# Changes of order and placement in a clustered-attention and SwiGLU kernel: casts of two heads, group and border order, table load, last output tile

## The chip, the cores and the metric

The kernel runs on one core of a Trainium2 chip. A core has five engines that run their own instruction streams in order and wait for each other on semaphores: TensorE (PE in the profile; its weight loads are shown as PEld), VectorE (DVE), ScalarE (ACT), GpSimd (POOL) and SyncE (SP), which here only issues DMAs. The metric is the time of one execution on the device, in microseconds. Lower is better.

## The reference

Attention over 4 batches, 8 heads, 768 tokens and 64 dimensions, restricted to pairs of tokens that fall into the same of 16 clusters, and behind it a normalised SwiGLU feed-forward layer:

```python
q_assign = argmax(einsum('bhsd,hcd->bhsc', q_n, c_n))
k_assign = argmax(einsum('bhsd,hcd->bhsc', k_n, c_n))
scores = where(q_assign[..., None] == k_assign[:, :, None, :], scale * q @ k^T, -1e9)
attn = softmax(scores) @ v
x = attn, heads side by side                  # 3072 x 512
xn = x / sqrt(mean(x*x) + 1e-6) * rms_g
out = (silu(xn @ w_gate) * (xn @ w_val)) @ w_out   # d_ff 1536
```

All inputs and the output are float32; the large products run in bf16.

## The kernel before

**Units and groups.** The 3072 tokens are cut into 8 *units* of 384 query tokens (half a batch each, three tiles of 128). Unit `u` goes through attention over 8 heads, then a norm, then the feed-forward layer. The 32 (batch, head) pairs are prepared in 8 *groups* of four heads: `trans` (L200) transposes q or k of one head on PE and evacuates it as `qkT` (ACT, or DVE for group 2); `cast` (L218) writes it as bf16 into `qext` or `kext`; `cluster_steps` (L254) finds the cluster of each token as one-hot rows, and `place` (L276) writes these rows by DMA below the 64 dimensions of `qext`/`kext`. A score product over 64 + 16 rows is then the scaled score plus a large number where the clusters agree; an exp with a bias takes the rest to zero. In the first two groups the one-hot rows are written by a DVE transpose instead (`pair_clusters`, `under`; `head(n)` does k and q of head `n`), and `cast` writes every second column there.

**Stages.** While unit `u` is in attention, PE also does feed-forward work of units `u-1` and `u-2` and transposes of a later group. `attention` (L591) walks over the 24 gaps of a unit (8 heads, three score chunks each): it issues the scores of a chunk (two 384-column matmuls and one exp on ACT), the product with v of the previous head (`pv`, L322, once per head; every second head DVE takes a reciprocal and writes `x`, which frees the accumulator), any hook for that gap, and then items from a list `fill`, spread by their costs. In unit 0 the hooks (`first`, with `gap1`, `gap5` and so on) carry the preparation of groups 0 to 2 instead. `gap5` (L565) has POOL cast k and q of heads 6 and 7; `head(6)` and `head(7)` follow in gaps 10 and 13, the transposes of group 2 (`late`, evacuated by DVE) in gaps 14 to 21. `second_batch` issues input loads on SP behind a small DMA (`hold`) that waits for a reciprocal of unit 0.

**The feed-forward work** of a unit (`ffn_work`) is four x transposes `xtrans` (L371; three PE transposes each, DVE writes `xnT`) and 12 pairs of gate and val (`gv`, L382): four 384-column matmuls each; ACT makes tanh of the gate, DVE two more steps (`th`, `gvT`); the last unit uses ACT's Silu and one DVE step. `out_work` is nine parts, three for each of three output tiles `o` (`out_mm`, L407; four 512-column matmuls per part), then ACT copies the tile to `o_sb` and SP issues its DMA. `border` puts the four x transposes of one unit between the last parts of the output work of the unit before. `CUT` leaves the last 8 of the 24 gate and val items of a unit to the start of the next unit.

**What sets the order.** The program is written in order by hand; each engine runs its instructions in that order. All transposes, gates, vals, cluster products and output tiles share three PSUM buffers (`ps_g`), scores have two, `pv` one. An instruction that needs a buffer waits for the engine that reads the oldest one.

**Behind the last attention gap** stand, in order: the last `pv`; the 8 left-over gates and vals of unit 6; the norm of unit 7 (three squares on ACT, a chain of small DVE steps, three DVE multiplications `xn`); the output of unit 6 with the x transposes of unit 7; gates and vals of unit 7; its output, whose last tile is copied in two halves by DVE and by ACT.

Of the kernel before, what the change touches and what calls it, by code (L numbers as in the profile page):

```python
# [9 lines left out]
F32 = mybir.dt.float32  # L10
# [4 lines left out]
ACT = mybir.ActivationFunctionType  # L15
# [7 lines left out]
def kernel(  # L23
# [12 lines left out]
    nc = tc.nc  # L36
    B, H, S, D = q.shape
# [238 lines left out]
    def place(on, g, m):  # L276

        ext = (kext if m else qext)[g % 4]
        for h in range(HG):
            for e in range(2):  # L280
                on.dma_start(out=ext[D:D + NC, h, e * UQ:(e + 1) * UQ],  # L281
                             in_=put[g, m][32 * h + e * NC:32 * h + (e + 1) * NC])
# [39 lines left out]
    def pv(u, h):  # L322
        b, _, nt = UNITS[u]
        g, hh = b * 2 + h // HG, h % HG
        if h == 0:
            xs[u] = xp.tile([P, HT, DM], F32, tag="x", name="x", bufs=2)
        if h % 2 == 0:
            accs[u] = ps_a.tile([P, 2, HT, D + 1], F32, tag="acc", name="acc")
        acc = accs[u]
        for t in range(nt):  # L330
            for kc in range(ST):
                nc.tensor.matmul(acc[:, h % 2, t], lhsT=pT[u, h][:, kc, t * P:(t + 1) * P],  # L332
                                 rhs=vbf[g % 4][:, hh, kc % HT * 2 + kc // HT], start=kc == 0, stop=kc == ST - 1)
        if h % 2:
            inv = small.tile([P, 2, HT], F32, tag="inv", name="inv")
            invs[u] = inv
            nc.vector.reciprocal(inv[:, :, :nt], acc[:, :, :nt, D])
            dst = xs[u][:, :nt, (h - 1) * D:(h + 1) * D].rearrange("p t (h d) -> p h t d", d=D)
            nc.vector.tensor_tensor(dst, acc[:, :, :nt, :D],
                                    inv[:, :, :nt].unsqueeze(3).broadcast_to([P, 2, nt, D]), op=ALU.mult)  # L340
# [63 lines left out]

    outs = {}

    def out_mm(u, t, part):  # L407
        b, col, _ = UNITS[u]
        if part == 0:
            outs[u] = ps_g.tile([P, DM], F32, tag="gen", name="o")  # L410
        for f in range(4 * part, 4 * part + 4):
            nc.tensor.matmul(outs[u], lhsT=gvT[u][:, f, t * P:(t + 1) * P], rhs=wo[:, f], start=f == 0, stop=f == FC - 1)  # L412
        if part == 2:
            o = outp.tile([P, DM], F32, tag="o_sb", name="o_sb")
            rows = out[b * S:(b + 1) * S].rearrange("(p t) f -> p t f", t=ST)[:, (col + t) % HT * 2 + (col + t) // HT]
            if (u, t) == (NU - 1, HT - 1):
                c = DM // 2
                nc.vector.tensor_copy(o[:, :c], outs[u][:, :c])
                nc.sync.dma_start(out=rows[:, :c], in_=o[:, :c])
                nc.scalar.copy(o[:, c:], outs[u][:, c:])  # L420
                nc.scalar.dma_start(out=rows[:, c:], in_=o[:, c:])
            else:
                nc.scalar.copy(o, outs[u])  # L423
                nc.sync.dma_start(out=rows, in_=o)


    def group_work(g):

        t, c = [], []
        for h in range(HG):  # L430
            n = g * HG + h
            t += [(0.3, lambda h=h: trans(g, h, 0)), (0.3, lambda h=h: trans(g, h, 1))]

            def others(n=n):
                vcast(n)
                load_qk(n + NQ)
                load_v(n + NV)

            def both(h=h, f=others):
                cast(nc.gpsimd, g, h, 0)  # L440
                f()
                cast(nc.vector, g, h, 1, (0,))
            if g == 2:
                c.append((0.0, others))
            else:
                c += [(0.0, both), (0.0, lambda h=h: cast(nc.vector, g, h, 1, (1,)))]
        a = []
        for m in range(2):
            a += [(0.0 if i else 0.7, f) for i, f in enumerate(cluster_steps(g, m))]
            a.append((0.0, lambda m=m: place(nc.sync if g == 2 else nc.gpsimd, g, m)))  # L450
        return t, c, a

    def group(g):
        t, c, a = group_work(g)
        return [x for h in range(HG) for x in t[2 * h:2 * h + 2] + c[2 * h:2 * h + 2]] + a

    def spread(a, b):

        if not a:
            return list(b)  # L460
        w, n = [], 0
        for i, x in enumerate(a):
            w.append(x)
            while n < len(b) * (i + 1) // len(a):
                w.append(b[n])
                n += 1
        return w

    def ffn_work(u):
        n = UNITS[u][2] / HT  # L470
        w = [(0.18 * n, lambda c=c: xtrans(u, c)) for c in range(CC)]
        for f in range(FC):
            for val in (False, True):
                w.append((0.64 * n, lambda f=f, val=val: gv(u, f, val)))
        return w
# [3 lines left out]

    def border(o, ffn):  # L480

        return o[:-3] + ffn[:2] + o[-3:-2] + ffn[2:3] + o[-2:-1] + ffn[3:4] + o[-1:]


    def tokens(g, h, on=None):
# [3 lines left out]
    def casts(on, n, *what):  # L489
        for m, e in what:  # L490
            cast(on, n // HG, n % HG, m, (e,))
# [39 lines left out]
    def more():  # L531
        busy(1, False)
# [10 lines left out]
    def head(n):  # L543
        under(n, 1)
        under(n, 0)
# [18 lines left out]

    def gap5():  # L565
        pair_clusters(2)
        casts(pool_, 6, K0, K1, Q0)
        casts(pool_, 7, K0, K1, Q0)
        vcast(6)
        vcast(7)  # L570
        load_gv(3)
        for n in (6, 7):
            casts(pool_, n, Q1)
        head(4)

    def gap9():
# [3 lines left out]
    early = [lambda h=h, m=m: trans(1, h, m) for h in (2, 3) for m in (1, 0)]  # L580
    late = [lambda h=h, m=m: trans(2, h, m, nc.vector) for h in range(HG) for m in (1, 0)]
    first = {1: gap1, 2: early[0], 3: early[1], 4: lambda: (early[2](), early[3]()), 5: gap5,
             7: lambda: (more(), head(5)), 9: gap9, 10: lambda: (more(), head(6)), 13: lambda: (more(), head(7))}
    first.update({14 + i: f for i, f in enumerate(late)})
    first[14] = lambda: (late[0](), second_batch())
    first[16] = lambda: (late[2](), casts(pool_, H, K0, Q0, K1, Q1))
# [4 lines left out]
    def attention(heads, fill, skip=0, hooks={}):  # L591
        gaps = [(u, h, i) for u, h in heads for i in range(UNITS[u][2])]
        total, done, n = sum(c for c, _ in fill), 0.0, 0
        for at, (u, h, i) in enumerate(gaps):
            scores(u, h, i)
            if i == min(1, UNITS[u][2] - 1):
                for p in due:
                    pv(*p)
                due[:] = [(u, h)]
            if h == H - 1:  # L600
                squares(u, i, False)
            if (u, h, i) in hooks:
                hooks[u, h, i]()
            while n < len(fill) and at >= skip and done <= total * (at + 1 - skip) / (len(gaps) - skip):
                done += fill[n][0]
                fill[n][1]()
                n += 1
        for _, f in fill[n:]:
            f()

    attention([(0, h) for h in range(H)], [], hooks={(0, *divmod(i, HT)): first.get(i, more) for i in range(H * HT)})
    for u in range(1, NU):
        ffn, o, g = ffn_work(u - 1), out_work(u - 2) if u > 1 else [], u + 2
        if u == 1:
            t, c, a = group_work(2)
            t3, c3, a3 = group_work(3)
            n = 4
            prep = c + a + [x for h in range(HG) for x in t3[max(2 * h, n):2 * h + 2] + c3[2 * h:2 * h + 2]] + a3[:5]
            idle = const.tile([P, 1], BF16)

            def norm():
                rms(0)
                nc.gpsimd.tensor_copy(idle, xn[0][:, HT - 1, DM - 1:])
                for h in range(1, HG):
                    casts(pool_, H + h, K0, Q0, K1, Q1)
                    load_o((h - 1) * FC // 3)

            hooks = {(1, 0, 1): norm}
            hooks.update({(1, *divmod(2 + i, HT)): t3[i][1] if i < n else more for i in range(LEAD - 2)})
            at = (1, *divmod(LEAD - 1, HT))  # L630
            hooks[at] = lambda f=hooks[at]: (f(), busy(4, False))
            fill = ffn[:CC] + spread(ffn[CC:CUT], prep)
            attention([(1, h) for h in range(H)], fill, LEAD, hooks)
        else:
            fill = ffn_work(u - 2)[CUT:] + [(0.0, lambda u=u: rms(u - 1))]
            fill += border(spread(o[:3], a3[5:]) + o[3:], ffn) if u == 2 else border(o, ffn)
            attention([(u, h) for h in range(H)], fill + spread(ffn[CC:CUT], group(g) if g < NG else []), 1)
    pv(NU - 1, H - 1)
    for _, f in ffn_work(NU - 2)[CUT:]:
        f()  # L640
    rms(NU - 1)
    for _, f in border(out_work(NU - 2), ffn_work(NU - 1)) + ffn_work(NU - 1)[CC:] + out_work(NU - 1):
        f()


# [28 lines left out]
```

## Time and profile before

| | |
|---|---|
| median of 6 runs | 355.77 us (355.05 to 356.78) |
| the profiled execution | 356.0 us, span 354.2 us |
| granted PE clock | 0.998 over the span |
| PE busy | 340.5 us (96%) |
| ACT busy | 261.3 us (74%) |
| DVE busy | 222.9 us (63%) |
| POOL busy | 112.5 us (32%), nearly all before 250 us |

The span is the time from the first to the last instruction in the profile; 1.8 us of the execution lie around it. In a row of the timeline or of the chain, the first number is the start in us from the beginning of the span, the second the duration; `x4` is the number of instructions that were merged; a bracket gives the time that the engine was idle before the row and what ended the idle time. `L412` is line 412 of the kernel before. A busy PE is not a PE at its peak: matmuls overlap, so a pause is seen where the distance between two starts is longer than usual. Unit 1 begins near 37.6 us and unit 2 near 79; from border to border a unit takes about 41.4 us while groups are being prepared and 36.9 us after that; the last attention gap is near 310 us.

### The profile page before, as it was taken

To read this page: it belongs to the slowest core of one execution; us is meant where nothing else is said; L and a number is where in the kernel's file an instruction comes from. 1 tells how busy PE (TensorE), PEld (TensorE's weight loads), DVE (VectorE), ACT (ScalarE), POOL (GpSimd) and SP (SyncE) were. 2 spreads that over 40 slices of the span, in tenths; PEclk is the share of its full clock that TensorE was granted. 3 is DMA by queue.
4 is the path that set the end of the run, shared out by engine and by line. 5 is a ranking of instruction groups with operands and counts; after the bars stand their busy time and mean duration, and the time that the engine had idled before them with its cause. 6 is when DMAs were issued, how large, how long until landed. Compare 5 with 4: busy or idle time off the path is not lost.

```text
span 354.2 us, 7973 instructions
## 1 busy us (share of the span) xinstructions
PE 340.5 (96%) x3016; PEld 207.8 (59%) x3033; DVE 222.9 (63%) x549; ACT 261.3 (74%) x458; POOL 112.5 (32%) x226
## 2 busy tenths in 40 slices
PE   7997999999999999999999999999999999999995
PEld 3646656565665557655675656755566656654552
DVE  3887869677568655786368764687546654675430
ACT  5897968987778769787787877878778877852421
POOL 4899586241453403371042801535000000000000
PEclk9999999999999999999999999999999999999999
DMA  7999989273361014501130001000100001001002
GB/s 261 333 227 196 304 155 270 63 219 116 98 192 40 17 59 138 162 16 39 59 92 2 22 32 61 0 9 18 59 31 0 2 35 57 3 0 62 30 2 89
DMA packets 27158, 31.62 MB, mean 89 GB/s; under 512 B 4464, under 2 KB 24176, under 8 KB 27120
## 3 DMA queue, kind: packets, MB, share of 16 engines
q1 hardware_dynamic: 18320, 24.88, 21.2%
q0 software_dynamic: 8368, 5.71, 9.8%
q8 instruction: 24, 0.39, 0.5%
q10 hardware_dynamic: 432, 0.52, 0.4%
q14 instruction: 14, 0.11, 0.1%
HBM read 28.35 MB, written 6.29 MB: 98 GB/s over the span
## 4 chain that ended last, share of the span: by engine, by line
PE 81%; ACT 9%; DVE 3%; DMA 2%; issue 2%; POOL 2%; SPq 0%; ACTq 0%; DVEq 0%; POOLq 0%
PE o L412 17%; PE gate L390 16%; PE val L390 15%; PE s L314 15%; PE acc L332 9%; ACT pT L318 5%; PE tq L206 4%; PE sc L240 3%; DMA qk<-in_q_dram 1%; PE tx L377 1%; ACT th L398 1%; ACT qkT L212 1%; POOL qext L225 1%; ACT xn L357 1%; DMA out_dram<-o_sb 1%
## 5 line engine op out<-in xcount | busy, mean ns | idle before, releaser
L318 ACT ACTIVATE pT<-s,off 128x768 bf16<-128x768 f32 x192 | 171.0, 904 | 36.2 <-PE s L314 35.3
L314 PE MATMUL s<-qext,kext 80*128 80x384 bf16 x384 | 94.8, 327 | 4.2 <-POOL qext L225 1.6
L390 PE MATMUL gate<-xnT,wg 128*128 128x384 bf16 x384 | 78.3, 325 | 0.4 <-DVE gvT L403 0.4
L390 PE MATMUL val<-xnT,wv 128*128 128x384 bf16 x384 | 78.1, 326 | 0.5 <-ACT th L396 0.5
L399 DVE SCALAR_TENSOR_TENSOR th<-th,gate 128x384 f32<-128x384 f32 x84 | 46.5, 554 | 50.2 <-ACT th L398 49.7
L412 PE MATMUL o<-wo,gvT 128*128 128x512 bf16 x271 | 69.2, 378 | 1.2 <-ACT o_sb L423 0.3
L225 POOL CAST qext<-qkT 64x384 bf16<-64x384 f32 x64 | 34.4, 543 | 77.3 <-ACT qkT L212 34.7
L314 PEld LDWEIGHTS <-kext 80*128 80x128 bf16 x384 | 36.9, 98 | 35.8 <-issue 10.7
L398 ACT ACTIVATE th<-gate 128x384 f32<-128x384 f32 x84 | 41.1, 489 | 16.6 <-PE gate L390 16.2
L390 PEld LDWEIGHTS <-wv 128*128 128x128 bf16 x384 | 36.1, 97 | 25.3 <-issue 3.3
L403 DVE SCALAR_TENSOR_TENSOR gvT<-th,val 128x384 bf16<-128x384 f32 x84 | 46.1, 549 | 6.8 <-PE val L390 1.5
L390 PEld LDWEIGHTS <-wg 128*128 128x128 bf16 x384 | 35.8, 97 | 24.1 <-issue 3.1
L332 PEld LDWEIGHTS <-pT 128*128 128x128 bf16 x1152 | 43.6, 97 | 9.3 <-ACT pT L318 0.6
L332 PE MATMUL acc<-vbf,pT 128*128 128x65 bf16 x1152 | 45.7, 193 | 0.5 <-ACT pT L318 0.5
L412 PEld LDWEIGHTS <-gvT 128*128 128x128 bf16 x288 | 26.9, 97 | 26.1 <-issue 0.5
L206 PE MATMUL tq<-ident_f,qk 128*128 128x128 f32 x192 | 31.5, 280 | 1.5 <-DMA qk<-in_q_dram 1.3
L212 ACT ACTIVATE qkT<-tq 128x384 f32<-128x384 f32 x56 | 26.6, 496 | 4.5 <-PE tq L206 4.0
L281 POOL DMA_DIRECT2D qext<-oh x40 | 19.1, 486 | 30.3 <-DVE oh L270 24.3
L206 PEld LDWEIGHTS tq<-ident_f,qk 128*128 128x128 f32 x192 | 23.1, 142 | 9.4 <-DVE gvT L403 1.8
L423 ACT COPY o_sb<-o 128x512 f32<-128x512 f32 x23 | 13.5, 585 | 19.6 <-PE o L412 19.2
L378 DVE TENSOR_SCALAR xnT<-tx,gcol 128x384 bf16<-128x384 bf16 x32 | 12.7, 414 | 22.7 <-PE tx L377 22.5
L281 POOL DMA_DIRECT2D kext<-oh x40 | 19.1, 485 | 11.2 <-DVE xnT L378 10.9
(71 smaller groups left out, 250.9 us busy)
## 6 DMA issues: line engine op xcount, KB each, us to landing
qk<-in_q_dram SPq DMA_DIRECT2D x32, 192.0 KB, 3.9
vs<-in_v_dram SPq DMA_DIRECT2D x32, 192.0 KB, 4.6
out_dram<-o_sb SPq DMA_DIRECT2D x23, 256.0 KB, 2.0
qk<-in_k_dram SPq DMA_DIRECT2D x30, 192.0 KB, 4.1
wg<-in_moe_w_gate_dram POOLq DMA_DIRECT2D x4, 384.0 KB, 7.4
wv<-in_moe_w_val_dram POOLq DMA_DIRECT2D x4, 384.0 KB, 9.1
wo<-in_moe_w_out_dram POOLq DMA_DIRECT2D x3, 512.0 KB, 5.9
qext<-oh POOLq DMA_DIRECT2D x40, 12.0 KB, 1.6
```

Of the source, the lines that this page charges most:

```text
L206: nc.tensor.transpose(ps[:, i * P:(i + 1) * P], qk[:, part, 2 * i:2 * i + 2].rearrange("p t d -> p (t d)"), ident_f)
L212: nc.scalar.activation(to, ps, ACT.Copy, scale=by)
L225: on.tensor_copy(to, of)
L281: on.dma_start(out=ext[D:D + NC, h, e * UQ:(e + 1) * UQ], in_=put[g, m][32 * h + e * NC:32 * h + (e + 1) * NC])
L314: nc.tensor.matmul(ps[:, j, :w] if nt == HT else flat[:, j * w:(j + 1) * w], lhsT=cols(kext[g % 4][:KR, hh], g, kc // HT, kc % HT * P, (kc ...
L318: nc.scalar.activation(pT[u, h][:, n * i:n * i + n, :w], of, ACT.Exp, bias=off, scale=scale * ZS)
L332: nc.tensor.matmul(acc[:, h % 2, t], lhsT=pT[u, h][:, kc, t * P:(t + 1) * P], rhs=vbf[g % 4][:, hh, kc % HT * 2 + kc // HT], start=kc == 0 ...
L390: nc.tensor.matmul(ps, lhsT=w[:, c, f * P:(f + 1) * P], rhs=xnT[u][:, c, :n], start=c == 0, stop=c == CC - 1)
L398: nc.scalar.activation(th, ps, ACT.Tanh, scale=0.5)
L399: nc.vector.scalar_tensor_tensor(th, th, 1.0, ps, op0=ALU.add, op1=ALU.mult)
L403: nc.vector.scalar_tensor_tensor(gvT[u][:, f, :n], gates[u], 0.5, ps, op0=ALU.mult, op1=ALU.mult)
L412: nc.tensor.matmul(outs[u], lhsT=gvT[u][:, f, t * P:(t + 1) * P], rhs=wo[:, f], start=f == 0, stop=f == FC - 1)
```

## The change

Five places of the program are changed.

- k of heads 6 and 7 is cast by DVE behind `head(6)` in gap 10 and `head(7)` in gap 13, instead of by POOL in gap 5.
- For groups 4 to 7, `place` for q no longer stands behind the cluster steps of q; one item behind those of k places both. The list of a group has one entry less, and so the interleave with the gates and vals shifts.
- `border` puts the first part of the third output tile ahead of the x transposes: two transposes follow it, then the second part, two transposes, and the third part.
- One gate of unit 6 is put ahead of the last `pv`. A dummy Silu behind the last norm brings the load of ACT's table there.
- The last output tile is computed in two column halves, each with 12 matmuls of 256 columns in a PSUM tile of its own; ACT copies the first half, DVE the second, and SP issues both DMAs.

```diff
     def out_mm(u, t, part):
...
-            if (u, t) == (NU - 1, HT - 1):
-                c = DM // 2
-                nc.vector.tensor_copy(o[:, :c], outs[u][:, :c])
-                nc.sync.dma_start(out=rows[:, :c], in_=o[:, :c])
-                nc.scalar.copy(o[:, c:], outs[u][:, c:])
-                nc.scalar.dma_start(out=rows[:, c:], in_=o[:, c:])
-            else:
-                nc.scalar.copy(o, outs[u])
-                nc.sync.dma_start(out=rows, in_=o)
+            nc.scalar.copy(o, outs[u])
+            nc.sync.dma_start(out=out_rows(u, t), in_=o)
+
+    def out_half(u, t, half):
+
+        c = slice(half * DM // 2, (half + 1) * DM // 2)
+        to = ps_g.tile([P, DM // 2], F32, tag="gen", name="o")
+        for f in range(FC):
+            nc.tensor.matmul(to, lhsT=gvT[u][:, f, t * P:(t + 1) * P], rhs=wo[:, f, c], start=f == 0, stop=f == FC - 1)
+        o = outp.tile([P, DM // 2], F32, tag="o_sb", name="o_sb")
+        if half:
+            nc.vector.tensor_copy(o, to)
+        else:
+            nc.scalar.copy(o, to)
+        nc.sync.dma_start(out=out_rows(u, t)[:, c], in_=o)
...
             a += [(0.0 if i else 0.7, f) for i, f in enumerate(cluster_steps(g, m))]
-            a.append((0.0, lambda m=m: place(nc.sync if g == 2 else nc.gpsimd, g, m)))
+            if g <= 3:
+                a.append((0.0, lambda m=m: place(nc.sync if g == 2 else nc.gpsimd, g, m)))
+        if g > 3:
+            a.append((0.0, lambda: [place(nc.gpsimd, g, m) for m in range(2)]))
...
     def border(o, ffn):
 
-        return o[:-3] + ffn[:2] + o[-3:-2] + ffn[2:3] + o[-2:-1] + ffn[3:4] + o[-1:]
+        return o[:-2] + ffn[:2] + o[-2:-1] + ffn[2:4] + o[-1:]
...
     def gap5():
         pair_clusters(2)
-        casts(pool_, 6, K0, K1, Q0)
-        casts(pool_, 7, K0, K1, Q0)
+        casts(pool_, 6, Q0)
+        casts(pool_, 7, Q0)
...
-             7: lambda: (more(), head(5)), 9: gap9, 10: lambda: (more(), head(6)), 13: lambda: (more(), head(7))}
+             7: lambda: (more(), head(5)), 9: gap9, 10: lambda: (more(), head(6), casts(nc.vector, 6, K0, K1)),
+             13: lambda: (more(), head(7), casts(nc.vector, 7, K0, K1))}
...
+    rest = ffn_work(NU - 2)[CUT:]
+    rest[0][1]()
     pv(NU - 1, H - 1)
-    for _, f in ffn_work(NU - 2)[CUT:]:
+    for _, f in rest[1:]:
         f()
     rms(NU - 1)
-    for _, f in border(out_work(NU - 2), ffn_work(NU - 1)) + ffn_work(NU - 1)[CC:] + out_work(NU - 1):
+    nc.scalar.activation(first_exp, off, ACT.Silu)
+    for _, f in border(out_work(NU - 2), ffn_work(NU - 1)) + ffn_work(NU - 1)[CC:] + out_work(NU - 1)[:-3]:
         f()
+    for half in range(2):
+        out_half(NU - 1, HT - 1, half)
```

More of the change, by code (lines that the diff above doesn't have):

```diff
@@ L405, with out_rows @@
     outs = {}
+    def out_rows(u, t):
+        b, col, _ = UNITS[u]
+        return out[b * S:(b + 1) * S].rearrange("(p t) f -> p t f", t=ST)[:, (col + t) % HT * 2 + (col + t) // HT]
     def out_mm(u, t, part):
-        b, col, _ = UNITS[u]
         if part == 0:
@@ L414, in out_mm @@
             o = outp.tile([P, DM], F32, tag="o_sb", name="o_sb")
-            rows = out[b * S:(b + 1) * S].rearrange("(p t) f -> p t f", t=ST)[:, (col + t) % HT * 2 + (col + t) // HT]
-            if (u, t) == (NU - 1, HT - 1):
-                c = DM // 2
-                nc.vector.tensor_copy(o[:, :c], outs[u][:, :c])
-                nc.sync.dma_start(out=rows[:, :c], in_=o[:, :c])
-                nc.scalar.copy(o[:, c:], outs[u][:, c:])
-                nc.scalar.dma_start(out=rows[:, c:], in_=o[:, c:])
-            else:
-                nc.scalar.copy(o, outs[u])
-                nc.sync.dma_start(out=rows, in_=o)
+            nc.scalar.copy(o, outs[u])
[11 more added lines that the diff above has]
+        nc.sync.dma_start(out=out_rows(u, t)[:, c], in_=o)
     def group_work(g):
```

## The prediction

> **What bounds the kernel now.** I read the page's shares and chain first, then the chain of waits in order of time near the end, then the timeline of the stretches that the edits touch.
>
> ```profile
> PE 81%; ACT 9%; DVE 3%; DMA 2%; issue 2%; POOL 2%; SPq 0%; ACTq 0%; DVEq 0%; POOLq 0%
> ```
>
> TensorE (PE) is busy for 340.5 of 354.2 us and makes 81% of the chain that ended last. Whatever lies beside it is free; what counts is the short pauses in which PE waits. Start-to-start distances of its matmuls give the pauses: 0.163 us for a 384-column one, 0.2155 us for a 512-column one (22 in 4.92 us of the chain), 0.11 us for an f32 transpose; anything longer is a pause. The end of the chain shows four:
>
> ```profile
> 311.56 0.60 PE acc L332 x14
> ...
> 322.65 0.59 ACT o_sb L423
> 323.24 0.04 issue
> 323.29 1.02 PE o L412 x4
> ...
> 327.08 1.22 issue
> 328.30 0.50 ACT th L396
> 328.80 0.04 issue
> 328.85 0.81 PE val L390 x4
> ...
> 350.46 0.44 DVE o_sb L418
> 350.90 0.02 issue
> 350.92 0.37 ACT o_sb L420
> ```
>
> The last `pv` (`acc`) waits for the last exp; the third output tile waits for a PSUM buffer that ACT's copy frees; a gate waits for the Silu table (1.28 us of the "issue" row); and the two halves of the last copy run one after the other. The timeline of unit 3 has a smaller copy of the second, and one more kind:
>
> ```profile
> 128.32 0.59 ACT L423 COPY o_sb<-o 128x512 f32<-128x512 f32 x1 [0.83 <-PE o L412]
> ...
> 128.95 1.02 PE L412 MATMUL o<-wo,gvT 128*128 128x512 bf16 x3
> ...
> 144.88 0.31 PEld L206 LDWEIGHTS tq<-ident_f,qk 128*128 128x128 f32 x3 [0.37 <-DVE gvT L403]
> ```
>
> PE starts `o` right when the copy ends (128.91), and the transpose right when `gvT` (144.29 + 0.54) frees its buffer. In the head, the edit of the casts meets this:
>
> ```profile
> 30.37 0.31 PEld L206 LDWEIGHTS tq<-ident_f,qk 128*128 128x128 f32 x3 [0.53 <-DVE qkT L210]
> ...
> 30.54 1.31 POOL L225 CAST kext<-qkT 64x384 bf16<-64x384 f32 x2
> ...
> 32.57 0.50 PE L314 MATMUL s<-qext,kext 80*128 80x384 bf16 x2 [1.64 <-POOL qext L225]
> ```
>
> Scores of head 6 wait for POOL. DVE (VectorE) is then already late too: the fourth transpose waited for it until 30.37.
>
> **The change, part by part.** All on the profiled execution: span 354.2 us, its own time 356.0 us (1.8 us around the span), 0.23 above the median 355.77 of the six runs. I subtract the sum from the median.
>
> *Casts of k, heads 6 and 7.* POOL loses four casts (0.61 to 0.65 us each) and could give q of head 6 by 31.2 instead of 32.52. DVE gains four casts of c us: two ahead of the reciprocal at 27.75, two ahead of the `qkT` copy at 29.76. Queued behind the first two: reciprocal and `x`, which free the accumulator for the next `pv` (so PE stands 2c there), the `hold` DMA on SP and the loads behind it. Those land about 1 us later, which is covered: the load of head 12, issued at 28.65, lands 4.1 us later, and its transposes run at 39.8. Behind all four: the copy that frees the buffer of PE's fourth transpose. That transpose starts at 30.38 + 4c, takes 0.33, and the scores of head 6 follow at 30.71 + 4c. Against 32.57 that breaks even at c = 0.465. DVE's own contiguous cast takes 0.355 in most cases, 0.55 and 0.57 at 61.4 and 94.8 where a POOL cast ran beside it (gain 0.4, loss 0.4 us). These casts write every second column; on POOL that costs 0.61 against 0.50. POOL is casting beside the first two (27.50 to 29.13) and part of the others (from 30.54), so I take 0.50: **+0.1 us**, bounds -0.45 and +0.4. From there ACT's exps follow back to back to 40.9, so the shift goes through to the end. POOL's later work (weights issued 2.5 us earlier, first used tens of us later) gates nothing.
>
> [...]
>
> *Group work, units 2 to 5.* `place` of both halves behind the second half's steps leaves POOL's order as it was (eight DMAs of q, then eight of k). But the list is nine entries long instead of ten, so the interleave with gates shifts: by the instruction order the last head's two transpose triples stand together behind the gate, and on DVE `gvT` no longer stands behind a k cast that waits for ACT. The pauses at 103.47, 144.88, 186.36 and 227.77 (0.15, 0.15, 0.22, 0.15 us) should go: **-0.6 us**, bounds -0.67 and 0 (something else frees the buffer as late).
>
> *Third output tile ahead of the x transposes, units 2 to 7.* Its first part follows the second tile at once: of three PSUM buffers one is then free, and the copy of the second tile (0.59) lies under its 0.86 us. The same matmuls run, only reordered. The pauses of 0.17 us in units 3 to 7 (128.95, 170.37, 211.84, 254.46, 291.35) go; unit 2 has none: **-0.85 us**, bounds -0.85 and 0 (rival 3 is what could make it a loss). Next in line is the gate behind the last transposes: two `xnT` copies end 1.11 us after the transposes start (first copy 0.37 after, 0.74 for both), the gate starts 0.31 + 0.86 + 0.33 = 1.50 after. Covered.
>
> *Last unit.* The same swap removes its longer pause, 0.50 (323.29 against 322.79): **-0.5**, bounds -0.5 and -0.3, as there is no score pair here and the gate comes 1.17 after the transposes. The gate pulled ahead of the last `pv` fills PE's 0.63 us wait at 311.56. But its `th` now stands on DVE ahead of reciprocal and `x` (0.2 + 0.56), and this stretch of four gate/val pairs is DVE's as much as PE's (`th` and `gvT` start 0.65 apart from 313.37 to 317.96). Worked through: the gate starts at 310.81, ACT is busy with exp and squares until 312.0, tanh takes 0.49, `th` starts at 312.53, `x` ends 313.88, first `gvT` 314.45, so the third gate waits 0.5 for its buffer and the last val starts at 316.45 instead of 316.62: **-0.2**, bounds -0.63 and +0.1. The norm behind it needs no cover: PE now has seven output parts (6.0 us) over a chain of 3.7 us.
>
> *Silu table.* Its load moves to between the last squares (ACT done at 318.15) and the first output copy (320.06): 1.28 + 0.2 fit into that 1.9 us idle. The gate's activation then follows the copy of tile 3; val at 328.85, 0.69 late, starts on time: **-0.69**, bounds -0.69 and -0.4 (if the copy delays it). [...]
>
> *Two column halves.* 24 matmuls of 256 columns for 12 of 512: same columns, 2.59 us; the 0.163 us of 384 columns and 0.2155 of 512 extrapolate to 0.11 for 256, 2.65 us in all, so at most 0.06 more. The first half's copy and DMA lie under the second half. After the last matmul came DVE's copy, ACT's copy (350.92, behind DVE's), ACT's DMA issue (351.32), 1.7 us to landing; now only DVE's copy and SP's issue, which stood at 350.92: **-0.4**, bounds -0.45 and -0.3.
>
> Sum: +0.1 - 0.6 - 0.85 - 0.5 - 0.2 - 0.69 - 0.4 = -3.1 us. **352.6 us** from the median, a span near 351.1. All ends at their best give -4.2 (351.5), all at their worst -0.5 (355.3).
>
> **Rivals.**
> 1. *DVE becomes the bound of the head.* For: it already made PE wait at 30.37, and it takes work exactly there. Against: c must exceed 0.47. If strided and contended costs add up, c = 0.355 + 0.2 + 0.08 to 0.76, the loss is 0.7 to 1.2 us in place of 0.1: 353.2 to 353.7.
> 2. *The small pauses move, they don't go.* With three PSUM buffers a freed wait can return at the next allocation; then groups, borders and the moved gate bring nothing (+1.65): 354.3. For: buffers are freed by ACT and DVE, whose work is unchanged. Against: ACT shows idle time of 0.1 to 1.0 us in front of most exps of unit 3, so it can follow.
> 3. *Slower: the gate waits for the late `xnT`.* All four x transposes now come later, the last pair with one output part behind it. Price: DVE's lateness beyond the 0.39 us of cover in the units and 0.06 in the last, at seven borders. To end above 356.8 it must cost 0.6 us at each: DVE a full 1 us late each time, say with reciprocal and `x` (0.8) in front. Against: the `pv` just before those transposes in units 3 to 5 (130.14) has no reciprocal behind it, and DVE idled 0.6 to 1.1 us before each `xnT` copy.
>
> **How the numbers follow.** Forecast as summed 0.62 (own range 351.5 to 353.3); rival 1 0.13; rival 2 0.15; rival 3 0.05; anything unseen 0.05. About 0.3% (1.07 us) is what a measurement of this kernel can tell from no change: faster is below 354.7. Rival 2 with its spread gives most of "same". Faster 0.86, same 0.09, slower 0.05. The range reaches down to the best ends with the runs' scatter and up to rival 2: 351.2 to 354.4.
>
> **What would show it.** Scores of head 6 start near 32.7, and their wait names DVE or ACT, no longer POOL; k casts on DVE of 0.36 to 0.56; no `o` wait on `o_sb`, no val wait on a table; the load near 318; the last DMA issued 0.5 us after the last matmul, none on ACT's queue. I am wrong if gate rows name `xnT`, if units 2 to 5 keep their length (41.4 us from border to border), or if the first scores of unit 1 come over 0.5 us later than 37.65.

## The result, and the profile after

The changed kernel takes **354.26 us** (median of 21 executions, 353.87 to 355.40). The kernel before, measured beside it, takes 356.42 us (47 executions, 354.83 to 356.99). The ratio is 0.9952, 95% interval 0.9942 to 0.9962: 0.48% or 1.7 us faster, as the mean times have it too (354.42 against 356.13). The medians lie further apart, 2.2 us, because the times of before fall into two groups, as is shown below. The forecast was 3.1 us. So the direction was right and the time lies just inside the stated range (351.2 to 354.4), but only about half of the gain came.

The profiled execution of the changed kernel took 355.13 us, span 353.4 us. Two lines of its page answer to those of before: the clock granted to PE, in 40 slices of the span, and the shares of the chain that ended last.

```profile
PEclk9997899999999999999999999999999999999999
...
PE 84%; DVE 7%; ACT 6%; issue 1%; DMA 1%; DVEq 0%; ACTq 0%
```

"issue" and ACT have shrunk in the chain, as forecast. DVE has grown from 3% to 7%, and there is a dip in a line that the prediction never read: in the fourth and fifth slice the clock falls below full.

The chain in order of time, at the end of the same execution (start, duration, what):

```profile
311.72 0.92 ACT pT L318
...
315.32 0.81 PE gate L390 x4
316.13 0.65 PE val L390 x4
...
324.16 0.34 PE tx L377 x6
324.49 0.86 PE o L415 x4
...
327.85 0.65 PE gate L390 x4
328.50 0.65 PE val L390 x4
...
347.33 2.63 PE o L426 x24
349.97 0.04 DVEq L429
350.00 0.04 issue
350.05 0.42 DVE o_sb L429
```

The wait of a third output tile for `o_sb` is gone. A gate, a val and the next gate stand 0.65 us apart where the table load had opened a hole. After the last matmul there is one copy instead of two. ACT's own timeline shows where the table went: into the idle time behind the last squares.

```profile
318.63 0.19 ACT L357 ACTIVATION_READ_ACCUMULATOR xn<-x 128x1 f32 x1
318.84 1.28 ACT L656 ACT_TABLE_LOAD   x1
320.14 0.20 ACT L656 ACTIVATE first_exp<-off 128x1 f32<-128x1 f32 x1
320.74 0.58 ACT L418 COPY o_sb<-o 128x512 f32<-128x512 f32 x1 [0.40 <-PE o L415]
```

The head is another matter. Its timeline in the changed kernel (in brackets the idle time before, and what ended it):

```profile
28.76 0.72 PE L332 MATMUL acc<-vbf,pT 128*128 128x65 bf16 x18 [0.69 <-DVE x L339]
...
29.82 1.15 POOL L225 CAST qext<-qkT 64x384 bf16<-64x384 f32 x2
29.90 1.90 DVE L225 CAST kext<-qkT 64x384 bf16<-64x384 f32 x2
...
31.71 2.09 DVE L210 TENSOR_SCALAR qkT<-tq 128x384 f32<-128x384 f32 x4
...
32.30 0.90 PE L206 MATMUL tq<-ident_f,qk 128*128 128x128 f32 x3 [2.12 <-DVE qkT L210]
32.99 0.85 PE L314 MATMUL s<-qext,kext 80*128 80x384 bf16 x2
```

Two things are to be seen. PE stands 2.12 us for the `qkT` copy that is queued on DVE behind the casts (before, it stood 1.64 us for POOL). And the scores after that pause take 0.85 us for two matmuls that took 0.50 before: PE runs at half its clock (granted 0.50 from 31.69 to 38.52).

### Where the time went

To compare kernels, the span is cut at two matmuls: the first scores of unit 0, and the first x transpose in unit 1 (of unit 0's x). Between them lies the *head*, and behind them the *rest*. All are starts read from the timelines, in us.

| execution | first scores | head | rest | half clock |
|---|---|---|---|---|
| before, as shown to the forecast | 12.22 | 31.95 | 310.05 | none |
| changed | 11.30 | 35.73 | 306.32 | 6.83 us |
| change in rest and head | | +3.78 | -3.73 | |

The rest gained more than forecast (3.73 against 3.24, all terms but the casts). The head gave all of it back in this pair of executions, and the span is shorter only because the first scores came 0.92 us earlier. The experiments take these three apart.

### The profile page after: what moved, and what is told of

It is laid out like the page before. It is cut to its first block, busy times and chain, and to the rows that moved or that the text cites. A ratio compares the mean times of both kernels' runs of the same rounds, so it can differ in the third digit from the quotient of the medians.

```text
span 353.4 us, 7991 instructions
## 1 busy us (share of the span) xinstructions
PE 341.6 (97%) x3028; PEld 210.7 (60%) x3045; DVE 223.2 (63%) x553; ACT 261.6 (74%) x459; POOL 110.0 (31%) x222
## 4 chain that ended last, share of the span: by engine, by line
PE 84%; DVE 7%; ACT 6%; issue 1%; DMA 1%; DVEq 0%; ACTq 0%
PE gate L390 17%; PE o L415 17%; PE val L390 16%; PE s L314 16%; PE acc L332 9%; PE tq L206 5%; PE sc L240 3%; ACT pT L318 3%; PE tx L377 1%; DVE kext L225 1%; ACT xn L357 1%; DVE qext L298 1%; DVE kext L298 1%; ACT th L398 1%; PE o L426 1%
## 5 line engine op out<-in xcount | busy, mean ns | idle before, releaser
L314 PE MATMUL s<-qext,kext 80*128 80x384 bf16 x384 | 95.8, 331 | 2.3 <-ACT pT L318 1.5
L415 PE MATMUL o<-wo,gvT 128*128 128x512 bf16 x259 | 66.0, 379 | 0.9
L415 PEld LDWEIGHTS <-gvT 128*128 128x128 bf16 x276 | 25.8, 97 | 25.1
L206 PEld LDWEIGHTS tq<-ident_f,qk 128*128 128x128 f32 x192 | 24.2, 147 | 9.3 <-DVE qkT L210 2.7
```

Of the source, the lines that this page charges most:

```text
L206: nc.tensor.transpose(ps[:, i * P:(i + 1) * P], qk[:, part, 2 * i:2 * i + 2].rearrange("p t d -> p (t d)"), ident_f)
L314: nc.tensor.matmul(ps[:, j, :w] if nt == HT else flat[:, j * w:(j + 1) * w], lhsT=cols(kext[g % 4][:KR, hh], g, kc // HT, kc % HT * P, (kc ...
```

## The experiments

### Undoing the casts, and doing them alone

`casts_back` is the changed kernel with the casts as before; `casts_only` is the kernel before with this one edit:

```diff
     def gap5():
         pair_clusters(2)
-        casts(pool_, 6, K0, K1, Q0)
-        casts(pool_, 7, K0, K1, Q0)
+        casts(pool_, 6, Q0)
+        casts(pool_, 7, Q0)
...
-    ... 10: lambda: (more(), head(6)), 13: lambda: (more(), head(7))}
+    ... 10: lambda: (more(), head(6), casts(nc.vector, 6, K0, K1)),
+        13: lambda: (more(), head(7), casts(nc.vector, 7, K0, K1))}
```

> The changed kernel with the four k casts back on POOL in gap 5, everything else as changed. Theory (the cast edit alone eats half of the gain: in the changed kernel unit 0's x transposes start 2.9 us later while all that follows is 3.6 us shorter): first x transpose near 44 us as before, TensorE clock full throughout unit 0, time 3.2 to 3.8 us under the kernel before. Rival (the other edits are worth only the 1.7 us that was measured, the head's delay comes from elsewhere): no faster than the changed kernel, 1.5 to 2 us under the kernel before.

> The kernel before with only the four k casts moved to DVE. Theory: a loss of 1.5 to 2.5 us where the clock falls briefly and up to 3.8 us where it stays halved for 6.8 us; a cast on DVE of 0.6 us or more (one of 1.3) beside POOL's casts. Rival of the prediction (c = 0.50): a loss of 0.1 us, at most 0.4, and a full clock.

Measured: `casts_back` 353.05 us, ratio to before 0.9898 (0.9875 to 0.9921); `casts_only` 358.17 us, ratio 1.0049 (1.0032 to 1.0065). So the casts make the kernel slower, and without them the other four parts bring about 1.0%. The segments say the same: `casts_back` has the head of before (31.97) and the rest of after (306.37), `casts_only` a head of 34.54 and a rest of 310.14. In the profiled execution of `casts_only` the clock was halved for 3.41 us. What was expected of the clock of `casts_back`, that it stays full, held in its profile but in only two of its six executions (mean clock 0.999 and 1.0, the others 0.993 to 0.995); why is shown below.

### A pause without the half clock

`keep_warm` is the changed kernel with ten matmuls into a score buffer that nobody reads, placed where PE stands for DVE:

```diff
+    def warm_s(n):
+        to = ps_s.tile([P, 2, 512], F32, tag="s", name="warm")
+        for i in range(n):
+            nc.tensor.matmul(to[:, 0].rearrange("p (a b) -> p a b", b=P), lhsT=warm,
+                             rhs=warm.unsqueeze(1).broadcast_to([P, 4, P]), start=True, stop=True)
...
+    first[17] = lambda: (warm_s(10), late[3]())
```

> The changed kernel with ten spare 128x512 matmuls (2.2 us) in a scores buffer, put into the pause of TensorE in which the fourth transpose of group 2 waits for DVE. Casts and DVE order stay. Theory (pause plus halved clock): the clock stays full in unit 0, the time falls by 1 to 2 us against the changed kernel, and what is left of the loss is the wait of about 1.3 us. Rival (the halved clock costs nothing, since ACT's exps set the pace there; all the loss is DVE's wait): the clock stays full and the time is that of the changed kernel within 0.3 us.

Measured: 352.54 us, ratio 0.9889 (0.9869 to 0.9910), with the clock full in all five executions. The casts are the same (783 ns in the mean, 776 in the changed kernel) and so is the place of the late transpose, 21.03 us behind the first scores against 21.00. Yet the head is 33.02 instead of 35.73. So the head's loss has two parts: **1.07 us** of waiting for DVE (33.02 - 31.95), and the half clock, 2.7 us for 6.83 us of it here and 1.5 us for 3.41 us in `casts_only` (34.54 - 33.02).

Why the clock falls is seen when the span is cut at the moments at which it changes. In the changed kernel it was granted at 4.38 us, held for 27.31 us and was then halved for 6.83; 27.31 is 8 times 3.413, 6.83 twice. So I take stretches, *windows*, of 3.41 us counted from the grant. The columns are: window, length, then busy us (and instructions) of PE, PEld, DVE, ACT and POOL, the granted clock, the DMA share and GB/s. The changed kernel:

```profile
28.28:31.69 3.41, 1.42 (x23) 1.01 (x23) 3.34 (x5) 1.72 (x3) 3.41 (x7) 1.00 0.80 86
31.69:35.10 3.41, 2.80 (x14) 2.06 (x15) 2.55 (x6) 0.90 (x1) 3.31 (x6) 0.50 1.25 235
35.10:38.52 3.42, 3.42 (x30) 2.75 (x27) 1.67 (x5) 1.80 (x2) 1.66 (x4) 0.50 1.18 291
```

`keep_warm`, the same stretch behind its own grant:

```profile
29.22:32.63 3.41, 3.41 (x33) 1.96 (x33) 3.37 (x6) 1.23 (x2) 3.41 (x7) 1.00 0.81 98
```

With PE busy for 1.42 us of a window the next one ran at half clock; with 3.41 us it did not. The other 1.99 us are 0.48 of the pause of 0.69 and 1.51 of the pause of 2.12 (the rest of each lies outside the window). By these rows it is the empty share of one window that counts. The count does not start with the span: in three profiles of the kernel before (the other two follow below), it starts at 4.57, 4.93 and 6.68 us.

The second halving in the changed kernel followed the window from 31.69, which ran at half clock and had 2.80 us of PE work. The like window of `casts_only` had 3.25 us, and full clock came back behind it:

```profile
31.97:35.38 3.41, 3.25 (x22) 2.51 (x23) 2.15 (x5) 1.29 (x2) 3.31 (x7) 0.50 1.27 230
```

So a window at half clock needed more work here than one at full clock, for which the next section finds the bound.

### The kernel before again: start and clock are drawn anew

The remaining 0.92 us, the earlier first scores, could belong to the change or be scatter. Both kernels and `casts_back` were profiled once or twice more, unchanged.

> The kernel before, unchanged, to read one number: when the first score matmul starts. Theory A (the start scatters from execution to execution, with the pauses in SP's issue of the first loads, and is no part of the change): the first score can come anywhere between 11.1 and 13.0 us, and differs by over 0.3 us from the 12.22 of the first profile in this run or in the next; the time moves with it, the rest of the execution being 343.8 us (356.0 - 12.2). Theory B (the start belongs to the program): 12.2 +- 0.2 again, and about 356.0 us.

> The same once more. Theory A: a start that again differs from the others, time = start + 343.8 us. Theory B: 12.2 +- 0.2.

> The changed kernel, unchanged, for the same number (11.30 before) and for the head from the first score to the first x transpose. Theory A: a start between 11.1 and 13.0; B: 11.3 +- 0.2. The head should be 35.7 if the granted clock is halved for two windows (6.83 us) and 34.6 if for one (3.41 us), everything behind it 306.3.

> The changed kernel with k of heads 6 and 7 cast by POOL again, for the same number (13.00 before). Theory A: a start between 11.1 and 13.0, so 351.2 to 353.1 us; B: 13.0 +- 0.2 and 353.1 us. Head 31.95, everything behind it 306.4 by both.

| execution | time | first scores | head | half clock |
|---|---|---|---|---|
| before, first | 356.0 | 12.22 | 31.95 | none |
| before_again | 356.43 | 11.18 | 33.39 | 3.41 us |
| before_third | 357.25 | 11.99 | 33.42 | 3.41 us |
| after, first | 355.13 | 11.30 | 35.73 | 6.83 us |
| after_again | 354.90 | 11.19 | 35.60 | 6.83 us |
| casts_back, first | 353.12 | 13.00 | 31.97 | none |
| casts_back_again | 352.99 | 11.47 | 33.41 | 3.41 us |

The start scatters between 11.18 and 13.00 us, by over 1 us for one and the same kernel; for the start theory A holds, and the 0.92 us was no part of the change. Its times did not hold: it gave 355.0 us for `before_again` (11.18 + 343.8) and 355.8 for `before_third`, and each took 1.5 us more. What makes it scatter was not tried; SP's issue of the first loads pauses in different places (from 5.39 to 6.68 us in the first profile of before, from 3.50 to 4.26 in that of `casts_back`).

What no theory expected is the last column. The kernel **before** loses clock too, in two of three profiles. Its 1.64 us wait for POOL is the cause that the windows show; `k7_later` and `k6_pool_first` below, which do not have it, kept full clock in all nine executions. In the first profile of before (first row) a window ended at 31.88, inside the pause (30.93 to 32.57), and each half of the pause stood in a window with enough other work:

```profile
28.46:31.88 3.42, 2.34 (x29) 1.59 (x28) 3.18 (x7) 2.47 (x3) 3.33 (x6) 1.00 1.06 202
31.88:35.29 3.41, 2.72 (x34) 2.30 (x34) 1.49 (x4) 1.95 (x3) 3.26 (x7) 1.00 1.25 185
```

In `before_again` the same pause (29.87 to 31.52) lay inside one window:

```profile
28.82:32.23 3.41, 1.63 (x12) 0.99 (x10) 1.85 (x4) 1.17 (x3) 3.23 (x6) 1.00 0.92 179
32.23:35.65 3.42, 3.42 (x30) 2.74 (x28) 1.77 (x4) 1.98 (x3) 3.36 (x6) 0.50 1.23 214
```

I cut 13 profiles into such windows from end to end. Ahead of the last microseconds, eight windows at full clock had 1.29 to 1.77 us of PE work, and each was followed by half clock. The emptiest windows at full clock that kept it had 2.10 us (`casts_back`, from 29.49) and 2.13 us. So for a window at full clock the bound lies between 1.77 and 2.10 us here, some 52% to 62% of a window.

This explains why the times fall into groups. Each execution's mean clock tells its group: 0.998 or more, 0.993 to 0.995, or 0.989. Of the 23 executions of before beside the experiments, four kept the clock full (median 355.53 us) and 19 lost one window's worth (356.87). Of the changed kernel's 22, 15 lost one (354.15) and seven lost two (355.09); none kept it full.

Like with like, one window each, the change is worth 354.15 - 356.87 = -2.7 us. The segments give the same: -3.73 in the rest, +1.07 of waiting, +0.06 between the two windows' costs (1.52 and 1.46), -2.6 in all. The measured ratio is smaller because the change turns a frequent loss of clock into a certain one, and at times a double one. An estimate of this follows. Before: the times beside the changed kernel's fall into 20 up to 356.0 and 27 from 356.37; taking the upper group as the one that lost a window, the mean loss is 27/47 x 1.46 = 0.84. After: (15 x 1.52 + 7 x 2.65) / 22 = 1.88. Then -3.73 + 1.07 + 1.04 = -1.6 us, against -1.7 measured.

### Why the casts on DVE were dear

The four casts took 776 ns in the mean, by this group of the changed kernel (count, total us, mean ns of one, idle before):

```profile
L225 DVE CAST kext<-qkT 64x384 bf16<-64x384 f32 x4 | 3.1, 776 | 0.1
```

Singly they took 0.62, 0.59, 1.30 and 0.59. POOL was making casts beside every one of them, those of q (strided) mostly beside the first and third, those of v beside the second and fourth:

```profile
26.04 1.16 POOL L225 CAST qext<-qkT 64x384 bf16<-64x384 f32 x2
26.81 1.23 DVE L225 CAST kext<-qkT 64x384 bf16<-64x384 f32 x2
27.25 1.15 POOL L228 CAST vbf<-vs 128x384 bf16<-128x384 f32 x2
...
30.87 1.30 POOL L228 CAST vbf<-vs 128x384 bf16<-128x384 f32 x2
```

Is it the write to every second column, or POOL's casts beside them? `stride_probe` adds copies of the same shape behind the last output, whose results are not used: eight on DVE alone (four contiguous, four into every second column), three and three beside POOL's strided casts, three and three beside POOL's contiguous ones.

```diff
+    # DVE alone: 4 contiguous, 4 into every second column
+    # 3 + 3 beside eight POOL casts 64x384, strided
+    # 3 + 3 beside eight POOL casts 128x384, contiguous
```

> The changed kernel with copies of 64x384 f32 to bf16 added behind its last output, which change no output: on DVE four contiguous and four to every second column while POOL is idle, then three and three while POOL makes eight copies of 64x384 to every second column, then the same while POOL makes eight contiguous 128x384. Theory A (the stride costs, POOL adds): contiguous alone 0.36 us, strided alone 0.60, and over 0.6 beside POOL's strided copies. Theory B (only POOL beside it costs, as the prediction weighed it): strided alone 0.36 to 0.44, 0.55 to 0.57 beside POOL, contiguous or not.

The three stretches on DVE (start, total duration), and POOL beside the second:

```profile
351.15 3.14 DVE L667 CAST pdst<-psrc 64x384 bf16<-64x384 f32 x8
...
355.00 3.79 DVE L667 CAST pdst<-psrc 64x384 bf16<-64x384 f32 x6
...
361.42 3.22 DVE L667 CAST pdst<-psrc 64x384 bf16<-64x384 f32 x6
```

```profile
355.22 5.37 POOL L667 CAST pdst<-psrc 64x384 bf16<-64x384 f32 x8 [109.77 <-DVE psrc L673]
```

Alone, one takes 0.352 contiguous and 0.374 strided: the stride costs 0.02 us. In each of the two stretches beside POOL, DVE's first cast began ahead of POOL's first and took 0.31. Of the others, one of either kind takes 0.64 to 0.66 after one of 0.71 beside POOL's strided casts, and 0.54 to 0.56 beside the contiguous ones. So the price is set by what POOL does, not by the stride: theory A's 0.60 for the stride is refuted, and theory B's 0.55 to 0.57 held beside contiguous casts alone. The price is close to POOL's own 0.60 to 0.64 and 0.51 to 0.54.

DVE and POOL did not take turns by whole casts: POOL's strided casts start 0.67 to 0.70 us apart beside DVE's and 0.67 apart after the last of them, where 0.37 and 0.60 in turn would be 0.97. By what means POOL's casts slow DVE's, no run shows.

The cast of 1.30 us, which met two of POOL's in the kernel (29.82 to 30.97), took 1.30 to 1.32 in all seven traces that have these casts in this place. It did not recur in the probe, and its cause stays open. It weighs: the other three took 0.60 in the mean.

### One cast pair later, and one on POOL in time

If the casts of k of head 7 are what holds up the fourth transpose, they need only stand behind it. `k7_later`:

```diff
-             13: lambda: (more(), head(7), casts(nc.vector, 7, K0, K1))}
+             13: lambda: (more(), head(7))}
...
+    first[18] = lambda: (late[4](), casts(nc.vector, 7, K0, K1))
```

> The changed kernel with the two casts of k of head 7 behind the fifth qkT copy on DVE (gap 18) instead of ahead of the first. Theory (what hurts is what stands ahead of the qkT copies): the transposes wait for two casts only, scores of head 6 start about 1.9 us earlier than in the changed kernel, no or a shorter halving of the clock, 2 to 3.5 us under the changed kernel's slow executions. Rival (casts on DVE beside POOL slow the whole queue wherever they stand): within 0.5 us of the changed kernel.

Measured: **350.87 us**, ratio 0.9842 (0.9820 to 0.9865), full clock in all executions. The head is 31.46. The waits of its PE from 20 to 46 us (total, times, longest):

```profile
PE acc L332 <- DVE x L339: 0.7, 1, 0.7
PE s L314 <- ACT pT L318: 0.6, 2, 0.4
PE tq L206 <- DVE qkT L210: 0.4, 1, 0.4
```

The transpose still waits 0.4 us, and `acc` 0.7 us for the `x` that the first two casts push back. `k6_pool_first` keeps that and removes these too: k of head 6 goes back to POOL, ahead of q of head 7, and POOL's third weight load moves behind them; k of head 7 stays on DVE in gap 18.

```diff
     def gap1():
...
-        load_gv(2)
...
     def gap5():
         pair_clusters(2)
-        casts(pool_, 6, Q0)
+        casts(pool_, 6, K0, Q0, K1)
         casts(pool_, 7, Q0)
+        load_gv(2)
...
-             ... 10: lambda: (more(), head(6), casts(nc.vector, 6, K0, K1)),
+             ... 10: lambda: (more(), head(6)),
```

> The version with the casts of k of head 7 on DVE in gap 18, and k of head 6 back on POOL in the order k, q, k, ahead of the third weight load instead of behind it. DVE then has no cast ahead of any qkT copy. Theory (what counts is what stands ahead of the qkT copies on DVE and ahead of q of head 6 on POOL): the fourth transpose waits as little as in the kernel before, scores of head 6 start another 0.5 to 1 us earlier than with both casts of head 6 on DVE, 349.9 to 350.6 us where that version took 350.9. Rival (ACT's exps or POOL are then the bound): within 0.3 us of that version.

Measured: **350.60 us**, ratio 0.9826 (0.9810 to 0.9842), faster than both kernels. In time it is 0.27 us from `k7_later`, which the rival allowed. The head is what sets it apart, 30.61 against 31.46; in the profile the first scores came 0.45 us later (11.70 against 11.25). Neither wait is left, but which of the two moves gained it was not separated:

```profile
PE tx L377 <- DVE xn L367: 0.7, 3, 0.4
PE s L314 <- ACT pT L318: 0.6, 2, 0.4
```

### The group work and the gate

`groups_back` puts `place` of each half behind its own cluster steps again; `gate_behind_pv` leaves all gates of unit 6 behind the last `pv`.

```diff
 # groups_back
-            if g <= 3:
-                a.append((0.0, lambda m=m: place(nc.sync if g == 2 else nc.gpsimd, g, m)))
-        if g > 3:
-            a.append((0.0, lambda: [place(nc.gpsimd, g, m) for m in range(2)]))
+            a.append((0.0, lambda m=m: place(nc.sync if g == 2 else nc.gpsimd, g, m)))
 # gate_behind_pv
-    rest = ffn_work(NU - 2)[CUT:]
-    rest[0][1]()
     pv(NU - 1, H - 1)
-    for _, f in rest[1:]:
+    for _, f in ffn_work(NU - 2)[CUT:]:
```

> The changed kernel with place behind the steps of each half in groups 4 to 7, as before. Theory (the shifted interleave removed the pauses of 0.15 to 0.22 us): units 3 and 4 go from 41.04 back to 41.2 to 41.25, and the pauses of the transposes behind DVE return; from the first x transpose to the last scores 0.6 to 1.0 us longer. Rival (all of the 0.4 us that a unit gained comes from the third output tile): no change of these lengths.

> The changed kernel without the gate ahead of the last pv. Theory (prediction: 0.2 us, because th then stands on DVE ahead of reciprocal and x): from the last score matmul to the last x transpose 14.35 us in the changed kernel becomes 14.5 to 14.6. Rival (the wait of 0.63 us was filled in full): 14.9 to 15.0. Everything ahead of the last scores as in the changed kernel.

In `groups_back` (355.43 us, one execution) the stretch from the first x transpose to the last scores is 264.99 us against 264.09 after: the group work is worth 0.90, and its pause is back in unit 3. Units 3 and 4 take 41.25 and 41.31 us instead of 41.03 and 41.04. All of it comes at one place in each of units 2 to 5, ahead of the score pair of gap 19: 0.20, 0.21, 0.28 and 0.20 us. (Unit 2 of the kernel before begins at 69.8 us, not near 79.) In unit 3, first in `groups_back`, then in the changed kernel at the same place, where the six transposes follow the gate without a wait:

```profile
146.98 0.31 PEld L206 LDWEIGHTS tq<-ident_f,qk 128*128 128x128 f32 x3 [0.38 <-DVE gvT L403]
```

```profile
146.25 0.81 PE L390 MATMUL gate<-xnT,wg 128*128 128x384 bf16 x4
146.90 0.82 PE L206 MATMUL tq<-ident_f,qk 128*128 128x128 f32 x6
```

In `gate_behind_pv` (354.79 us, one execution) the last scores and the last x transpose are 14.81 us apart instead of 14.35: the gate is worth 0.46. Its wait for the last exp is back:

```profile
311.87 0.60 PE L332 MATMUL acc<-vbf,pT 128*128 128x65 bf16 x14 [0.48 <-ACT pT L318]
```

## Why the prediction was right or wrong

| term | forecast, us | measured, us | from |
|---|---|---|---|
| casts of k | +0.1 (-0.45 to +0.4) | +1.07, and 1.5 or 2.7 of clock | head, `keep_warm`, `casts_only` |
| group work | -0.6 | -0.90 | `groups_back` |
| third tile, units | -0.85 | -0.84 | 265.83 to 264.99, before to `groups_back` |
| last border | -0.5 | -0.48 | 15.29 to 14.81, before to `gate_behind_pv` |
| gate ahead of `pv` | -0.2 | -0.46 | `gate_behind_pv` |
| Silu table | -0.69 | -0.68 | last x transpose to last val, 17.04 to 16.36 |
| two halves | -0.4 | -0.37 | last val to the end, 11.89 to 11.52 |

**Five terms held within their bounds, and one came out larger than its bound.** The borders, the table and the halves are right to 0.03 us; these were read as distances between starts in the trace, with the cover named. The gate was undersized: its step let the third gate wait 0.5 us for its buffer, and it waited 0.24 (it starts at 315.32 in the chain, right behind `gvT`, where the val in front of it would have let it start at 315.08). The group work brought 0.23 more than its four pauses of 0.67, which were its bound. The rest lies right behind each pause: in `groups_back` the transposes that waited take 0.38 us to the next matmul (146.98 to 147.36), and after the change each three take 0.33 there. The step priced the pause alone.

**Rival 3 did not happen** (no gate waits for `xnT`), nor rival 2: the pauses went and did not return.

**The step that failed is "Casts of k", in two ways.** First, c = 0.50. The formula of the step came out near: fourth transpose at 30.38 + 4c, scores 0.33 behind it. With the measured 0.776 it gives a loss of 4c - 1.86 = 1.24, and the runs have 1.07. But c was taken from two casts of 0.55 and 0.57 that had met POOL's shorter casts of 0.50 to 0.52 for nearly all of their time, and then set lower still, because some cast would not meet POOL. In this stretch every cast met POOL's, and three of them took 0.59 to 0.62, 0.60 in the mean. Four of 0.60 would give a loss of 0.5; the rest of the 1.24 is the one cast of 1.30, whose cause is open.

Rival 1 named the right bound, DVE in the head, and a right price, 0.7 to 1.2 us, and got 0.13. The price was in part luck: it added a cost of the stride, which the probe puts at 0.02, and the mean of 0.776 comes up to its upper end of 0.76 only by the cast of 1.30.

Second, and larger, the sum had no term for PE's clock. The prediction treated a pause as costing its own length. Here a pause also decides whether the next 3.41 us run at half clock, which cost 1.5 us here, and 1.1 more where a second one followed. This was to be read, if not priced: the six times before fell apart into 355.05 to 356.0 and twice over 356.7, which the forecast took as scatter, and the profile shown was of the group with full clock. The prediction's own test did say it: the first scores of unit 1 came at 40.52, not "over 0.5 us later than 37.65" but 2.9 later.

## What to carry to other kernels

Price a wait on PE at its length plus a possible window of half clock (1.5 us here), and look whether the clock line of several executions, not one, is full; here two groups of times were the sign that it wasn't. Before work is moved to DVE, look whether POOL is busy in just that stretch, and cost each piece at no less than POOL's duration, not at DVE's best (0.35 to 0.37 alone in the probe; here 0.61 each would have given a loss of 0.6 of the 1.07 us). And when only one edit of a bundle touches a stretch that is already late, look first at what is queued behind it: moving one pair of casts behind one transpose turned 0.5% into 1.6%.

## What the runs showed of the hardware that was not expected

- PE's granted clock changed only in steps of 3.413 us from the grant, in all 13 profiles (27.31 us are eight steps, 6.83 two). A window at full clock with 1.29 to 1.77 us of PE work was followed by half clock, one with 2.10 us or more was not; the same pause of 1.64 to 1.65 us did it or not by where it lay in a window. A window at half clock with 2.80 us was followed by a second one (`after`), one with 3.25 us was not (`casts_only`).
- A 64x384 cast on DVE took 0.35 to 0.37 us alone, contiguous or strided, 0.64 to 0.71 beside POOL's strided casts and 0.54 to 0.56 beside POOL's contiguous ones, while POOL's own starts kept nearly their pace (0.67 to 0.70 us apart, and 0.67 without DVE).
- The first scores of one unchanged kernel came between 11.18 and 12.22 us in three executions.
